# A gated two-layer expert kernel: weights loaded as blocks of adjacent rows, a half weight in a buffer of its own, and the work between the two expert layers rearranged

## The chip, the cores and the metric

One core of one Trainium2 chip. The metric is the device time of one execution in microseconds (us), the median of several runs. A profiled execution of the same kernel gives its own time, and the span from its first to its last instruction. Engine names: PE is the matrix engine (PEld its weight load), DVE the vector engine, ACT the scalar engine, POOL the third elementwise engine, SP the engine whose queue issues most of the transfers.

## The reference

Three parts run one after the other on 2304 tokens (4 batches of 576) of width 512.

```python
# 1: attention over the 32 largest scores of each row; 4 batches, 8 heads, 576 rows, 64 wide
scores = scale * q @ k.T ; keep the 32 largest of each row ; softmax ; attn @ v
# 2: soft mixture: 8 experts of 4 slots each (32 slots)
logits = x @ phi                              # 2304 x 32
d = softmax(logits, axis=0) ; slot_input = d.T @ x      # 32 x 512
for e in range(8):
    h = np.maximum(slot_input[e] @ w1[e], 0.0)          # 4 x 1024
    slot_out[e] = h @ w2[e]                             # 4 x 512
c = softmax(logits, axis=1) ; x = c @ slot_out          # 2304 x 512
# 3: gated mixture: the two best of 8 experts for each token
logits = x @ w_gate ; noise_scale = log1p(exp(x @ w_noise))
noisy = logits + noise_scale * noise ; top2, top2_w = two largest, their softmax
for e in range(8):
    h = np.maximum(x[mask] @ u1[e], 0.0) ; out[mask] += top2_w * (h @ u2[e])
```

(u1 and u2 stand for the third part's own w1 and w2, as in the kernel.) Each of the 32 weight matrices has 2 MB (512x1024 or 1024x512 float32).

## The kernel before, in words

*Attention* takes the first 420 us. It is one pipeline of 144 steps. During it five of the first weights are loaded in quarters, and the first half of the last w2 into `wz`.

*The soft mixture* (`moe`, lines 815 to 960): the eight w1 are read by PE as the wide operand (L860; 8 products of 4 column groups each for one expert), then the result `hs` is copied out of PSUM (L863 by ACT, L910 by DVE), turned (L851) and masked into `hM`. The eight w2 follow (L936; the last expert, in halves of the width, L940). Experts 0 to 6 add up in `sx`, which ACT copies to `sos`; the last one's two halves are added by DVE (L944). `sos` is turned and summed over the groups (L957) into `soT` (L964), the 32 slot outputs with their 512 features on partitions. `hs`, `hM` and `sos` all lie in the buffer `wb0`.

A contraction over 512 or 1024 rows goes in chunks of 128 rows, one row to a partition. Before, chunk c holds rows 128c to 128c+127: a partition's share of a weight is 4 pieces of 4 KB (w1, u1) or 8 pieces of 2 KB (w2, u2), taken from rows that lie 128 apart.

*The gates* (lines 1033 to 1111): `soT` times the gate weights (L1033), spread by group (`ggd`, L1038), times the softmaxed `c`, turned by `turn_c` into `ct` (L922, L923), gives the logits of all tokens (L1043). ACT and DVE work out the noisy logits and the two best (up to `mb`, L1079). PE counts positions (L1087 to L1093). Meanwhile PE multiplies `soT` with u1 of expert 0 (`weigh01`, L1004), since a token's input is a weighted sum of the 32 slot outputs. Where PE would wait it runs dummy products (`warm`, L846). Afterwards `gw`, the two gate weights of a token, are worked out (L1104, L1105 on DVE, L1108 on POOL), written into the rows `RW` and stored to the DRAM table `XD` (L1110), from which later experts fetch their tokens.

*The compaction* (`compact`, lines 1217 to 1238): for each of 18 token tiles a one-hot matrix is made, by DVE (L1231) or, for the tiles in `ONACT`, by two passes of ACT (L1226, L1227), and PE gathers expert 0's tokens with it (L1235). The first three quarters of u1 of expert 1 (`weigh01(1, c, P1)`) stand ahead of it on PE, the last quarter behind it. Then ACT rounds the first u2 (L1354), ACT and DVE copy the gathered tokens (`cts0`, L1256, L1257), and the first product of the gated experts can start (L1341, `first(0)`; it also needs `gs`, four small transfers issued by `stacked_g(0)`).

*The gated experts* (`gated`): 64 steps of products of three rounded parts (L1365 to L1367) until the end.

*Weight loads*: `order` lists the 32 weights, `slot` the buffer of each, `more(end)` issues the next loads as long as their buffer is free, `used` frees one. All go through SP's queue, in order: a load whose buffer is not yet free holds up whatever is behind it. Before, the loads around the change come in this order: w2 of experts 3, 4, 5, 6, the second half of the last w2 (into `wx1`), u1 of experts 0 and 1, the first quarter of u2 of expert 0, `gs`, the other quarters, u1 of experts 2 and 3, u2 of expert 1.

Of the kernel before, what the change touches and what calls it, by code (L numbers as in the profile page):

```python
# [34 lines left out]
ONACT = (7, 11, 15)  # L35
# [7 lines left out]
def moe_after_topk_attention(ctx: ExitStack, tc: tile.TileContext, q, k, v, phi, w1, w2, wg, wn, noise, u1, u2, qk, vt, qr, out):  # L43
# [3 lines left out]
    def pool(name, bufs=1, stack=ctx, **kw):  # L47
# [70 lines left out]

    def wload(i, part=None):
        m, e = order[i]  # L120
        h = homes[slot[i]]
        if (m, e) not in WT:
            WT[m, e] = wpool[h if h in wpool else h[:2]].tile([128, 4096], F32, name=h)
            held[slot[i]] = (m, e)
        if i == 15:
            whalf(1, WT[m, e][:, 0:2048])
            return
# [45 lines left out]


# [4 lines left out]
    def make_xtr(wk, xk, ps, soon, row, warm):  # L179
# [93 lines left out]
        def rest(b):  # L273
# [3 lines left out]
            A.copy(si[r], p[r])  # L277
# [35 lines left out]
        def last():  # L313
# [59 lines left out]
    def attention(st):  # L373
# [248 lines left out]
        def prepare():  # L622
# [3 lines left out]
            for i, w in enumerate((wg, wn)):  # L626
                at(40 + 2 * i, nc.sync.dma_start, wgn[:, :, 8 * i:8 * i + 8], w.rearrange("(c p) e -> p c e", p=128))
# [84 lines left out]
    def attention_check(st):  # L712
# [6 lines left out]
        c3 = st.tile([128, NT], I32, name="chk3")  # L719
# [95 lines left out]
    def moe(st, xp, xs, fast):  # L815
# [5 lines left out]
        for i in range(4):  # L821
            wpool[f"wy{i}"] = pool(f"wy{i}", 1, ta_st)
        tb = pool("tb", 1, tb_st, side="right")
# [32 lines left out]
        for e in range(E):  # L856
            w = WT[0, e].rearrange("p (c f) -> p c f", c=4)
            for n in range(2):
# [3 lines left out]
                if e == E - 1 and n == 0:  # L862
                    A.activation(hs[:, 0:512], h1[0], AF.Copy, scale=zs)  # L863
            used(0, e)
            more(20)
            if e == 5:
# [5 lines left out]
                if fast:  # L872
# [5 lines left out]
                    RW = tb.tile([128, 2, TT, ROW], F32, name="RW")  # L878
                    for c in range(2):
                        G.tensor_copy(RW[:, c, :, 0:NS], cn)  # L880
                        G.tensor_copy(RW[:, c, :, NS:NS + 1], ids.unsqueeze(2))
                        G.memset(RW[:, c, :, NS + 2:], 0.0)
# [27 lines left out]
        V.tensor_scalar(hs[:, 512:1024], h1[1], zs, None, op0=OP.mult)  # L910
# [7 lines left out]
        def turn_c():  # L918
            cf = cn.rearrange("p t s -> p (t s)")
            x = halves()  # L920
            for g in range(4):
                T.transpose(x[:, 0, g * 128:g * 128 + 128], cf[:, g * 128:g * 128 + 128], identf)  # L922
            T.transpose(x[:64, 1, :128], cf[:, 512:576], identf)  # L923
            A.copy(ct[:, 0:4], x[:, 0].rearrange("p (a b) -> p a b", a=4))
            A.copy(ct[:64, 4], x[:64, 1, :128])
# [3 lines left out]
        for e in range(E):  # L929
            w = WT[1, e].rearrange("p (c f) -> p c f", c=8)  # L930
            for n in range(2) if e == E - 1 else (None,):
                for c in range(8):
                    g = c % 4
                    o = slice(32 * g, 32 * g + 32)
                    if n is None:
                        T.matmul(sx[o], hM[:, e, c], w[:, c], start=(e == 0 and c < 4), stop=(e == E - 2 and c >= 4),  # L936
                                 tile_position=(0, 32 * g))
                    else:
                        x = wz.rearrange("p (c f) -> p c f", c=4)[:, c] if c < 4 else w[:, c - 4]
                        T.matmul(so[n][o, :256], hM[:, e, c], x[:, n * 256:n * 256 + 256], start=(c < 4), stop=(c >= 4),  # L940
                                 tile_position=(0, 32 * g))
                if e == E - 1:
# [36 lines left out]
        def stacked_g(e):  # L979
# [4 lines left out]
            for a in range(1, 4) if e == 0 else ():  # L984
                wload(18, a)
# [49 lines left out]
        if fast:  # L1035
            warm(2, "acc3")
# [8 lines left out]
        if fast:  # L1045
# [3 lines left out]
            warm(8, "acc2")  # L1049
# [54 lines left out]
        V.tensor_scalar(gw[:, 0], gw[:, 1], 1.0, 1e-9, op0=OP.add, op1=OP.add)  # L1104
        V.reciprocal(gw[:, 0], gw[:, 0])  # L1105
        wh_ = wpool["wx"].tile([128, 4096], F32, name="wx0")
        wf_ = wpool["wx"].tile([128, 4096], F32, name="wx1")
        G.tensor_tensor(gw[:, 1], gw[:, 1], gw[:, 0], op=OP.mult)  # L1108
# [548 lines left out]
```

## Time and profile before

| | us |
|---|---|
| median of 3 runs (741.35 to 742.44) | 741.62 |
| the profiled execution's own time | 739.92 |
| its span | 738.1 |
| PE busy in the span | 722.6 (98%) |
| DVE, ACT, POOL busy | 562.7, 484.8, 501.4 |

The time of the profiled execution is the span and 1.8 us around it. A busy time is the sum over an engine's instructions; PE's products are pipelined and their ends are modelled, and the dummy products count as busy, so 98% doesn't mean that PE does useful work in 98% of the time. "Idle before" in a row is the time that the engine stood still just ahead of it, with what ended it. The granted PE clock is 0.997 of full speed over the span.

### The profile page before, as it was taken

The numbers are of one execution on the slowest core, as the hardware profiler recorded it, in microseconds if no ns is written. First come the engines' busy times: TensorE is split into PE (matmuls) and PEld (weight loads), VectorE is DVE, ScalarE is ACT, GpSimd is POOL, SyncE is SP. The second block draws the span as 40 slices with busy tenths as digits, with TensorE's granted clock in tenths as the row PEclk, the third lists the DMA queues.
The fourth block names the chain that finished last, engine by engine and source line by source line (L and its number), as shares of the span: only waits on it lengthen the run. The fifth ranks groups of instructions, "written<-read, shape, count | busy, mean of one in ns | idle before, by whom it ended". The sixth has DMA issues, their size and how long they took to land.

```text
span 738.1 us, 17487 instructions
## 1 busy us (share of the span) xinstructions
PE 722.6 (98%) x5713; PEld 595.3 (81%) x5713; DVE 562.7 (76%) x2708; ACT 484.8 (66%) x1029; POOL 501.4 (68%) x656
## 2 busy tenths in 40 slices
PE   9999999999999999999999999999999999999995
PEld 4689999898999889998989634767876788888884
DVE  7999999999999998999987332978655656555561
ACT  5999999999999999999998302725222222322321
POOL 4999999998999999999877040436570527244044
PEclk9999999999999999999999999999999999999998
DMA  6147778776776543553376799999484986344055
GB/s 227 38 125 217 201 200 230 204 211 166 215 222 192 144 115 94 130 141 94 84 272 211 260 382 378 315 357 384 111 186 150 302 283 90 55 73 63 1 66 71
DMA packets 62326, 133.98 MB, mean 182 GB/s; under 512 B 13330, under 2 KB 14226, under 8 KB 62226
## 3 DMA queue, kind: packets, MB, share of 16 engines
q1 hardware_dynamic: 55042, 121.93, 54.3%
q0 software_dynamic: 7184, 10.85, 10.2%
q8 instruction: 47, 0.77, 0.4%
q14 instruction: 53, 0.43, 0.2%
HBM read 85.02 MB, written 17.97 MB: 140 GB/s over the span
## 4 chain that ended last, share of the span: by engine, by line
PE 53%; DVE 27%; POOL 8%; issue 5%; DMA 3%; ACT 2%; SPq 0%; POOLq 0%
DVE c L519 10%; PE acc L1365 9%; PE acc L1366 9%; PE acc L1367 9%; DVE TH L550 6%; PE av L586 5%; POOL u L542 4%; DVE c L526 4%; PE S L480 3%; DMA wx<-in_moe_w_dram 3%; PE st L562 3%; DVE mx L522 3%; PE hp L1341 2%; POOL s L557 2%; PE st L563 1%
## 5 line engine op out<-in xcount | busy, mean ns | idle before, releaser
L519 DVE MAX8 c<-s 128x8 f32<-128x82 f32 (+1 forms) x1008 | 222.2, 230 | 4.1 <-ACT s L499 3.5
L542 POOL TENSOR_TENSOR u<-g,s 128x576 f32<-128x576 bf16 x144 | 187.6, 1303 | 9.6 <-ACT g L536 9.6
L586 PEld LDWEIGHTS av<-vb,et 128*128 128x128 f32 (+1 forms) x1590 | 164.2, 180 | 11.2 <-issue 8.3
L586 PE MATMUL av<-vb,et 128*128 128x65 f32 (+1 forms) x1590 | 172.0, 263 | 0.8 <-ACT et L569 0.8
L1378 POOL DMA_INDIRECT out_dram<-y,ii x40 | 66.6, 1665 | 112.9 <-issue 60.3
L1346 ACT ACTIVATE hh<-hp 128x640 fp32r<-128x640 f32 x62 | 43.7, 705 | 136.1 <-PE hp L1341 132.6
L1365 PE MATMUL acc<-wh,hh 128*128 128x512 f32 x320 | 127.6, 399 | 0.8 <-DVE y L1375 0.7
L1366 PE MATMUL acc<-wl,hh 128*128 128x512 f32 x320 | 125.6, 393 | 0.0
L1367 PE MATMUL acc<-wh,hl 128*128 128x512 f32 x320 | 125.3, 392 | 0.0
L557 POOL TENSOR_SCALAR s<-s,mx 128x576 f32<-128x576 f32 x144 | 109.3, 759 | 21.3 <-ACT a L556 13.9
L550 DVE MAX8 TH<-u 128x8 f32<-128x584 f32 x144 | 109.2, 758 | 14.5 <-POOL u L543 13.6
L556 ACT ACTIVATE a<-s,TH 128x576 bf16<-128x576 f32 x144 | 117.6, 816 | 0.2
L536 ACT ACTIVATE g<-s,T 128x576 bf16<-128x576 f32 x144 | 116.6, 810 | 0.0
L562 PE MATMUL st<-identf,s 128*128 128x128 f32 x576 | 115.2, 280 | 1.3 <-POOL s L557 0.8
L1347 DVE SCALAR_TENSOR_TENSOR hl<-hp,hh 128x640 fp32r<-128x640 f32 x62 | 51.0, 823 | 75.1 <-ACT hh L1346 75.0
L563 PE MATMUL st<-steep,a 128*128 128x128 bf16 x576 | 105.5, 219 | 0.0
L480 PE MATMUL S<-ks,qs 128*128 128x288 f32 x560 | 105.1, 313 | 0.0
L501 ACT ACTIVATE s<-S 128x576 f32<-128x576 f32 x141 | 97.0, 688 | 4.8 <-PE S L490 2.8
L574 ACT ACTIVATE et<-st 128x512 f32<-128x512 f32 x144 | 90.6, 629 | 3.2 <-PE st L563 2.5
L562 PEld LDWEIGHTS st<-identf,s 128*128 128x128 f32 x576 | 83.5, 145 | 9.9 <-POOL s L557 3.3
L480 PEld LDWEIGHTS S<-ks,qs 128*128 128x128 f32 x560 | 78.6, 189 | 1.8
L1365 PEld LDWEIGHTS acc<-wh,hh 128*128 128x128 f32 x320 | 60.3, 189 | 15.1 <-issue 2.7
(368 smaller groups left out, 1158.1 us busy)
## 6 DMA issues: line engine op xcount, KB each, us to landing
wa<-in_moe_w_dram SPq DMA_DIRECT2D x8, 2048.0 KB, 13.4
wa<-in_moe_w_dram SPq DMA_DIRECT2D x28, 512.0 KB, 7.1
wb<-in_moe_w_dram SPq DMA_DIRECT2D x5, 2048.0 KB, 8.7
ks<-hl SPq DMA_DIRECT2D x56, 160.0 KB, 2.8
ks<-raw SPq DMA_DIRECT2D x56, 160.0 KB, 3.1
raw<-in_qk_dram SPq DMA_DIRECT2D x14, 608.0 KB, 4.2
wy<-in_moe_w_dram SPq DMA_DIRECT2D x4, 2048.0 KB, 10.6
wb<-in_moe_w_dram SPq DMA_DIRECT2D x16, 512.0 KB, 14.9
```

The source lines that it names most:

```text
L480: T.matmul(ph[hf][:, :288], QS[h][:, q0:q0 + 128], KS[h][:, l, ks], start=(n == 0), stop=(n == len(mm) - 1))
L519: V.max(C[i][:, c * 8:c * 8 + 8], SS[i][:, cut[c]:cut[c + 1]])
L536: A.activation(g, SS[i], AF.Sign, bias=last8(T24, i, 1), scale=-OVER, accum_out=SM[:, i:i + 1])
L542: G.tensor_tensor(u[:, 0:S], G1[i], SS[i], op=OP.mult)
L550: V.max(last8(TH, i), UU[i])
L556: A.activation(AP[i // 2][:, S * (i % 2):S * (i % 2) + S], SS[i], AF.Relu, bias=last8(TH, i, 1), scale=-1.0)
L557: G.tensor_scalar(SS[i], SS[i], -1.0, MX[i][:, 0:1], op0=OP.mult, op1=OP.add)
L562: T.matmul(o, SP[i // 2][:, ks], identf, start=True, stop=True, is_transpose=True)
L586: T.matmul(to[h][o:o + m, tt * 65:tt * 65 + 65], x, VB[j % 2][:, h, c if c < 4 else 4 + i % 2], start=(c == 0), stop=(c == 4), tile_positi ...
L1365: T.matmul(ACC[j], HH[n][:, r], WH[n], start=(c == 0), stop=False)
L1366: T.matmul(ACC[j], HH[n][:, r], WL[n], start=False, stop=False)
L1367: T.matmul(ACC[j], HL[n][:, r], WH[n], start=False, stop=(c == 7))
```

## The change

- Weights of w1, u1 and w2 are loaded in blocks of adjacent rows: of a block of 256 (w1, u1) or 512 rows (w2), partition p gets rows 2p and 2p+1, or 4p to 4p+3. A piece is then 8 KB. (The quarters loaded during attention stay at 4 KB; u2 keeps its layout.) w2 comes in two transfers instead of one.
- The other operand of each contraction has to follow that order of rows. The copies that already took it out of PSUM now deal it out: they read with a step of 2 or 4 elements (`dealt`, `taken`) in `rest`, in `last`, for `hs` and for `sos`. The gate weights are loaded in the same order, in two transfers each.
- The second half of the last w2 has a buffer of its own, `wv0` (8 KB of each partition), and is loaded right after w2 of expert 2. The last w2 is used first; the expert that is added in halves is now expert 6.
- u1 of experts 2 and 3 are loaded ahead of the first quarter of u2 of expert 0. u1 of expert 1 goes to `wx1`.
- `turn_c` is cut up: its transposes stand between the products that turn `sos` and behind L1033, in place of dummies.
- u1 of expert 1 is multiplied right behind that of expert 0, in place of eight dummies, and no longer around the compaction.
- `gw`, `RW`'s gate column and the store to `XD` come after the compaction. `RW` lies in `wb0` now, over `hM`, and is filled once `hM` is done with.
- `ONACT` is 8, 13, 17 instead of 7, 11, 15, with one scratch buffer `za` for all three. `ids_of(1)` comes two steps later.

```diff
-ONACT = (7, 11, 15)
+ONACT = (8, 13, 17)
...
-    order = ([(m, e) for m in range(2) for e in range(E)]
-             + [(2, 0), (2, 1), (3, 0), (2, 2), (2, 3), (3, 1), (2, 4), (2, 5), (3, 2), (2, 6), (2, 7)]
+    order = ([(0, e) for e in range(E)] + [(1, e) for e in (0, 1, 2, 7, 3, 4, 5, 6)]
+             + [(2, 0), (2, 1), (2, 2), (2, 3), (3, 0), (3, 1), (2, 4), (2, 5), (3, 2), (2, 6), (2, 7)]
...
-        f"wy{i}" for i in range(4)]
-    slot = [*range(11), 0, 1, 2, 3, 4] + [6, 0, 1, 2, 6, 5, 0, 2, 6, 1, 5] + [0, 2, 1, 5, 6]
+        f"wy{i}" for i in range(4)] + ["wv0"]
+    slot = [*range(12), 0, 1, 2, 3] + [6, 4, 0, 1, 2, 5, 6, 0, 1, 2, 5] + [6, 0, 2, 5, 1]
...
-            "(c p) f -> p c f", p=128))
+            "(p c) f -> p c f", p=128))
...
-        c = 4 if m % 2 == 0 else 8
-        n = 4 if m == 3 or part is not None else 1
-        d = WT[m, e].rearrange("p (c f) -> p c f", c=c)
-        s = (w1, w2, u1, u2)[m][e].rearrange("(c p) f -> p c f", p=128)
-        for a in range(n) if part is None else [part]:
-            cs = slice(a * c // n, (a + 1) * c // n)
-            nc.sync.dma_start(d[:, cs], s[:, cs])
+        s = (w1, w2, u1, u2)[m][e]
+        if h == "wv0":
+            whalf(1, WT[m, e])
+        elif m % 2 == 0:
+            d = WT[m, e].rearrange("p (a c f) -> p a c f", a=2, c=2)
+            s = s.rearrange("(a p c) f -> p a c f", a=2, c=2)
+            if part is None:
+                nc.sync.dma_start(d, s)
+            else:
+                nc.sync.dma_start(d[:, part // 2, part % 2], s[:, part // 2, part % 2])
+        else:
+            n = 2 if m == 1 else 4
+            d = WT[m, e].rearrange("p (a c f) -> p a c f", a=n, f=512)
+            s = s.rearrange("(a p c) f -> p a c f", a=n, p=128) if m == 1 else s.rearrange("(a c p) f -> p a c f", a=n, p=128)
+            for a in range(n) if part is None else [part]:
+                nc.sync.dma_start(d[:, a], s[:, a])
...
+    def dealt(x, a=1, c=2):
+        return x.rearrange("p (a c q) -> p a c q", a=a, c=c)
+
+    def taken(x, a=1, c=2):
+        return x.rearrange("p (a q c) -> p a c q", a=a, c=c)
...
-                copy(x[:, f], p[a][:, f])
+                copy(dealt(x[:, f]), taken(p[a][:, f]))
...
-                    A.activation(hs[:, 0:512], h1[0], AF.Copy, scale=zs)
+                    A.activation(dealt(hs[:, 0:512], 1, 4), taken(h1[0], 1, 4), AF.Copy, scale=zs)
...
-        V.tensor_scalar(hs[:, 512:1024], h1[1], zs, None, op0=OP.mult)
+        V.tensor_scalar(dealt(hs[:, 512:1024], 1, 4), taken(h1[1], 1, 4), zs, None, op0=OP.mult)
...
-        for e in range(E):
...
+        for e in (E - 1, *range(E - 1)):
...
-                    V.tensor_tensor(sos[:, f], so[n][:, 0:256], sos[:, f], op=OP.add)
-            if e == E - 2:
-                A.copy(sos, sx)
-                turn_c()
+                    V.tensor_tensor(dealt(sos[:, f]), taken(so[n][:, 0:256]), dealt(sos[:, f]), op=OP.add)
+            if e == E - 3:
+                A.copy(dealt(sos, 2), taken(sx, 2))
             used(1, e)
-            more(18 if fast else 20)
+            more(20)
         if fast:
-            wload(18, 0)
-            wnext[0] = 19
-        p = bank()
+            wload(20, 0)
+            wnext[0] = 21
+            RW = ww[:, F:F + 2 * TT * ROW].rearrange("p (c t f) -> p c t f", c=2, t=TT)
+            for c in range(2):
+                G.tensor_copy(RW[:, c, :, 0:NS], cn)
...
+        p, tc_ = bank(), halves()
         for c in range(4):
-            if c == 2 and fast:
-                warm(2, "acc3")
             T.matmul(p[:, c * 32:c * 32 + 32], sos[:, c * 128:c * 128 + 128], fold, start=True, stop=True)
+            if c == 1:
+                turn_c([0])
...
-        if fast:
-            warm(2, "acc3")
+        turn_c(range(1, 4))
...
-        if fast:
-            warm(2, "acc3")
+        turn_c([4])
...
-            warm(8, "acc2")
+            used(2, 0)
+            for c in range(4):
+                weigh01(1, c, P1)
+            used(2, 1)
...
-        used(2, 0)
-        more(21)
-        for c in range(3):
-            weigh01(1, c, P1)
         some(TT)
+        V.tensor_scalar(gw[:, 0], gw[:, 1], 1.0, 1e-9, op0=OP.add, op1=OP.add)
+        V.reciprocal(gw[:, 0], gw[:, 0])
+        G.tensor_tensor(gw[:, 1], gw[:, 1], gw[:, 0], op=OP.mult)
+        G.tensor_copy(RW[:, :, :, NS + 1], gw)
+        G.dma_start(XD[0:2 * NTOK].rearrange("(p r) f -> p (r f)", p=128), RW.rearrange("p c t f -> p (c t f)"))
         for e in (1, 0):
             slots_of(e)
-        weigh01(1, 3, P1)
-        used(2, 1)
```

## Rows read from the trace of the kernel before

**Rows 1.** The page: span, and PE's busy time with its share.
```profile
span 738.1 us, 17487 instructions
...
PE 722.6 (98%) x5713; PEld 595.3 (81%) x5713; DVE 562.7 (76%) x2708; ACT 484.8 (66%) x1029; POOL 501.4 (68%) x656
```

**Rows 2.** By stretch: start:end and length (us), PE busy (records), PEclk, DMA share, GB/s.
```profile
469.10:730.00 260.90, 259.89 (x1297) 1.00 0.64 168
```

**Rows 3.** The chain that ended last, in order of time: start, us, what.
```profile
428.37 19.36 DMA wx<-in_moe_w_dram
...
449.69 0.59 PE hp L922 x4
450.28 0.11 PE hp L923
...
452.82 0.43 PE acc L846 x2
...
453.61 0.43 PE acc L846 x2
...
454.44 0.54 PE acc L846 x2
454.98 1.32 PE acc L1043 x10
456.30 1.86 PE acc L1004 x32
458.16 1.83 PE acc L846 x8
...
468.56 0.57 PE tp L1004 x8
469.12 0.36 PE acc L1341
```

**Rows 4.** Timelines of PE (first row) and DVE: start, us, operation, count, idle before.
```profile
447.77 1.92 PE L936 MATMUL acc<-wx,wb 128*32 128x512 f32 x16 [0.21 <-DMA wx<-in_moe_w_dram]
...
452.32 0.42 DVE L944 TENSOR_TENSOR wb<-acc,wb 128x256 f32<-128x256 f32 x1 [0.37 <-PE acc L940]
...
454.52 0.22 DVE L1038 TENSOR_TENSOR ggd<-acc,group 128x64 f32<-128x64 f32 x1 [0.58 <-PE acc L1033]
...
459.41 0.31 DVE L1079 TENSOR_TENSOR mb<-T,nz 128x144 bf16<-128x144 f32 x1
...
499.67 0.59 DVE L1354 CAST wh<-wb 128x512 fp32r<-128x512 f32 x1
```

**Rows 5.** Timeline of ACT, around the end of the compaction.
```profile
466.61 0.74 ACT L1227 ACTIVATE wx<-wx 128x640 fp32r<-128x640 f32 x1
...
467.66 0.62 ACT L1354 CAST wh<-wa 128x512 fp32r<-128x512 f32 x1
468.45 0.43 ACT L1256 CAST cts<-acc 128x320 fp32r<-128x320 f32 x1 [0.16 <-PE acc L1235]
```

**Rows 6.** DVE groups by shape, 413 to 453 us: busy us, mean ns, idle before.
```profile
L325 DVE TENSOR_REDUCE mm<-st 1x32 f32<-1x160 f32 x1 | 0.3, 311 | 0.7 <-PE st L323 0.7
L910 DVE TENSOR_SCALAR wb<-acc,zs 128x512 f32<-128x512 f32 x1 | 0.8, 751 | 5.3 <-PE acc L860 5.3
```

**Rows 7.** By stretch, as rows 2: the transfers around the change.
```profile
419.00:423.00 4.00, 3.87 (x35) 1.00 0.16 58
439.00:447.00 8.00, 8.00 (x80) 1.00 1.05 386
450.00:457.00 7.00, 7.00 (x108) 1.00 1.03 421
461.00:465.00 4.00, 4.00 (x48) 1.00 0.58 151
```

**Rows 8.** Timeline of POOL.
```profile
462.41 1.01 POOL L1110 DMA_DIRECT2D xd<-RW  x1 [0.33 <-POOL RW L1109]
467.56 1.57 POOL L1158 TENSOR_SCALAR ge<-slot 128x18 f32<-128x18 f32 x6 [4.14 <-ACT slot L1229]
```

More of the change, by code (lines that the diff above doesn't have):

```diff
@@ L122, in wload @@
         if (m, e) not in WT:
-            WT[m, e] = wpool[h if h in wpool else h[:2]].tile([128, 4096], F32, name=h)
+            WT[m, e] = wpool[h if h in wpool else h[:2]].tile([128, 2048 if h == "wv0" else 4096], F32, name=h)
             held[slot[i]] = (m, e)
-        if i == 15:
-            whalf(1, WT[m, e][:, 0:2048])
-            return
-        c = 4 if m % 2 == 0 else 8
-        n = 4 if m == 3 or part is not None else 1
-        d = WT[m, e].rearrange("p (c f) -> p c f", c=c)
-        s = (w1, w2, u1, u2)[m][e].rearrange("(c p) f -> p c f", p=128)
-        for a in range(n) if part is None else [part]:
-            cs = slice(a * c // n, (a + 1) * c // n)
-            nc.sync.dma_start(d[:, cs], s[:, cs])
+        s = (w1, w2, u1, u2)[m][e]
[14 more added lines that the diff above has]
+                nc.sync.dma_start(d[:, a], s[:, a])
     def more(end, n=99):
@@ L276, in rest @@
             T.matmul(p[r], fold, SX[b], start=True, stop=True, tile_position=(0, 32 * b))
-            A.copy(si[r], p[r])
+            A.copy(dealt(si[r], 2), taken(p[r], 2))
         def merge1():
@@ L626, in prepare @@
             for i, w in enumerate((wg, wn)):
-                at(40 + 2 * i, nc.sync.dma_start, wgn[:, :, 8 * i:8 * i + 8], w.rearrange("(c p) e -> p c e", p=128))
+                for a in range(2):
+                    at(40 + 2 * i, nc.sync.dma_start, wgn[:, 2 * a:2 * a + 2, 8 * i:8 * i + 8],
+                       w[256 * a:256 * a + 256].rearrange("(p c) e -> p c e", c=2))
             for b in range(NB):
@@ L717, in attention_check @@
         V.scalar_tensor_tensor(c1, t24, 1.0, c1, op0=OP.is_lt, op1=OP.mult)
-        c3 = st.tile([128, NT], I32, name="chk3")
+        c3 = c2.bitcast(I32)
         V.tensor_scalar(c3, t24.bitcast(I32), 0x7fffff, None, op0=OP.bitwise_and)
@@ L822, in moe @@
             wpool[f"wy{i}"] = pool(f"wy{i}", 1, ta_st)
+        wpool["wv0"] = pool("wv0", 1, ta_st)
         tb = pool("tb", 1, tb_st, side="right")
@@ L877, in moe @@
                         G.tensor_copy(xw[:, :, 1, l], xw[:, :, 0, l])
[L878 to L882, printed above, removed]
             if e == 0:
@@ L916, in moe, with turn_c @@
         ct = tb.tile([128, 5, 128], F32, name="ct")
-        def turn_c():
+        def turn_c(gs):
             cf = cn.rearrange("p t s -> p (t s)")
[L920 to L925, printed above, removed]
+            for g in gs:
+                if g < 4:
+                    T.transpose(tc_[:, 0, g * 128:g * 128 + 128], cf[:, g * 128:g * 128 + 128], identf)
+                else:
+                    T.transpose(tc_[:64, 1, :128], cf[:, 512:576], identf)
+                if g == 3:
+                    A.copy(ct[:, 0:4], tc_[:, 0].rearrange("p (a b) -> p a b", a=4))
+                if g == 4:
+                    A.copy(ct[:64, 4], tc_[:64, 1, :128])
         sx, so = bank("acc2"), [bank(f"acc{n}") for n in range(2)]
         sos = ww[:, F + 2048:F + 2560]
-        for e in range(E):
-            w = WT[1, e].rearrange("p (c f) -> p c f", c=8)
-            for n in range(2) if e == E - 1 else (None,):
-                for c in range(8):
+        for e in (E - 1, *range(E - 1)):
+            if e == E - 1:
+                w = [x.rearrange("p (c f) -> p c f", c=4)[:, c] for x in (wz, WT[1, e]) for c in range(4)]
+            else:
+                w = [WT[1, e].rearrange("p (c f) -> p c f", c=8)[:, c] for c in range(8)]
+            for n, cs in ((0, range(4)), (1, range(4)), (0, range(4, 8)), (1, range(4, 8))) if e == E - 2 else (
+                    (None, range(8)),):
+                for c in cs:
                     g = c % 4
@@ L1103, in moe @@
         stacked_g(0)
[L1104 to L1105 removed]
         wh_ = wpool["wx"].tile([128, 4096], F32, name="wx0")
[L1107 to L1110 removed]
+        za = gp.tile([128, CAP], F32, name="za")
         idx = gp.tile([128, 2, TT], I32, name="idx")
@@ L1442, in gated @@
                 rows(1)
-                ids_of(1)
                 hots_of(t2, 0, (0, 1))
@@ L1452, in gated @@
                 rows(0)
+                ids_of(1)
                 ids_of(0)
```

17 lines of the change are left out of this document (8 added, 9 removed).

## The prediction, made before the changed kernel was built or run

> **What bounds the kernel now.** I read the page first: PE is busy in 722.6 of 738.1 us [rows 1]. That share can't be taken at its word, since dummy products count, so the next view is the chain that ended last [rows 3], and it shows three kinds of stretch. From 469.12 us on (the first product of the gated experts) PE works almost without a pause, 259.89 of 260.90 us [rows 2]; nothing in the change takes products out of that stretch, so it is moved as a block, and the question is by how much L1341 moves. Between the two expert layers, 447.77 to 469.12, the chain runs over short PE pieces, among them dummies (L846) and the transposes of `turn_c` (L922), and at its end over ACT. Ahead of 447.77 stands one long piece of DMA: the last full w2 (into `wx0`) landed 428.37 + 19.36 = 447.73. That looks like a transfer-bound stage, but PE's row there has only 0.21 us of idle time ahead of it [rows 4]; the two run level. The third view is the transfers by stretch [rows 7]: nearly nothing at 419 to 423 (58 GB/s), then full. Full means 386 GB/s where w2 in pieces of 2 KB moves and 421 GB/s where u1 in pieces of 4 KB does. At 461 to 465 it is down to 151 GB/s: there the next loads wait behind `gs`.
>
> So I sum what moves L1341, step by step along the chain, and then ask whether the transfers let it.
>
> **The sum, on PE's path**
>
> 1. `turn_c` leaves its old place: 0.59 + 0.11 [rows 3] = 0.70 us gained.
> 2. The wait for the last w2. `wv0`'s 1 MB goes out in the hole at 419 to 423 [rows 7] and no longer queues in the middle, and expert 6 is now used 1.8 us later. 0.2 us gained.
> 3. Turning `sos`. The second pair of L957 stood behind two dummies: 452.82 + 0.43 = 453.25 [rows 3]. DVE's sum that it needs ended 452.32 + 0.42 = 452.74 [rows 4]. With one transpose (0.59 / 4 = 0.15) in their place it starts at 452.97: 0.28 gained. The next two dummies (453.61, 0.43) become three transposes (0.45): nothing; they cover the copy of `soT`. Of the dummies behind L1033 (454.44, 0.54) one transpose remains, and L1043 is then held by `ggd`, ready at 454.52 + 0.22 = 454.74 [rows 4], where it started at 454.98: I take 0.1 of these 0.24, since a start follows a release by some 0.1 elsewhere. `ct`'s copies on ACT now start only after the third of these transposes; they take 0.59 and 0.26 by the length of the same operations before, and end some 0.2 ahead of need. 0.36 gained in all, 0 if that cover is gone.
> 4. Expert 1's products in place of eight dummies: as L1004's 32 records for expert 0, 1.86, against 1.83 [rows 3]. PE is free again at about the moment at which `mb` is ready (459.41 + 0.31 = 459.72 [rows 4]; PE's dummies end 459.99). 0.03 lost. Its weights must have landed by 458.16 - 1.26 = 456.9.
>
> PE's granted clock is 1.00 in all of rows 7; of the dummies that go, real products fill all but some 0.4 us, so I leave it there.
>
> Everything up to the position counts moves by 0.70 + 0.20 + 0.36 - 0.03 = 1.23. ACT's chain through the compaction hangs on those counts; still four copies of `gl` and three pairs, so it moves with them.
>
> 5. The end of the compaction. ACT ends its last pair at 466.61 + 0.74 = 467.35, rounds the first u2 from 467.66 (0.62), and then waited 0.16 for PE before `cts0` at 468.45 (0.43) [rows 5]. With the last tile on ACT and PE free of `weigh01(1, 3)`, PE has only that tile's two products to do behind ACT's last pair and is done before the rounding is. The 0.16 goes, and the 0.57 of L1004 at 468.56 [rows 3] with it, which only covered that copy. `cts0` then follows the rounding at once (468.28 instead of 468.45): 0.17 gained. DVE gives up the two `gw` operations ahead of its one-hots, but ACT ends last; nothing.
>
> 1.23 + 0.17 = 1.40 us.
>
> **What is moved elsewhere.** On POOL, filling `RW` (six short operations) moves to the end of the w2 products, where POOL has nothing to do; the `nt` that DVE needs for its one-hots is made behind it, some us ahead of need: nothing. `gw` and the store (1.01 [rows 8]) now stand ahead of `slots_of`, which began at 467.56; some 1.5 us later it still ends ahead of the joins on PE that read it, in steps 2 and 4 of the gated experts. The store lands later, about 473, but its first readers, the gathers of step 2, come after that. On SP the next load behind u2 of expert 0 is u2 of expert 1 into `wb0`, and it waits for that store; queued behind it are `gs` of expert 1 and u1 of experts 4 and 5. That u2 is first read at 499.67 [rows 4], over 25 us after the store, and its 2 MB take 5.4 at 386 GB/s: nothing.
>
> The strided copies: no row reads with a step of 2. The nearest is L325, which reads PSUM with a step of 32 elements: 311 ns for 160 elements [rows 6]; L944, contiguous, takes 0.42 for 256 [rows 4] and L910 751 ns for 512 [rows 6], the same 1.2 to 1.3 ns an element between them. So I take nothing for them. From below: no reason for a gain. From above: double the time for those on the path (the copy in `last`, as long as L944: 0.42; L910's 0.75; the second L944, 0.42), 1.6 us.
>
> On the layout in PSUM the Trainium skill speaks against the change: "SBUF — State Buffer", section "Door 1: The DMA port swizzle", says that PSUM has lines of 8 bytes, two fp32 values, and that a non-contiguous pattern slows matmuls significantly. It gives no price for a copy by DVE or ACT; L325's row shows none.
>
> **Do the transfers let it?** From `wv0` on, the queue is never empty until u2's first quarter and `gs` have landed. Before, the four w2 of experts 3 to 6 came first in it, and the last landed at 447.73; at 386 GB/s their 8.39 MB take 21.7, so that, with start-up and lag, they count from 426.0. With `wv0` running ahead there is less start-up, and I take 425.5. Then come 8 weights in pieces of 8 KB, 16.78 MB, and 0.52 MB each of u2's quarter (386 GB/s: 1.36) and `gs` (about 1.3). Needed: the quarter at 467.66 - 1.23 = 466.4, `gs` at 469.12 - 1.40 = 467.7.
>
> No row shows pieces of 8 KB. Bounds: 386 if they bring nothing over 2 KB, and 441 if the step from 386 to 421 is a fixed cost for a piece (5.31 ns for 2 KB and 9.73 for 4 KB over all engines: 0.88 fixed, so 18.6 for 8 KB). I take 430, between 4 KB's row and that.
>
> - 430: 39.0 us; the quarter lands 465.9, `gs` 467.2. In time by 0.5.
> - 421: 39.9; 466.8 and 468.1. L1341 0.4 late: gain 1.0.
> - 386: 43.5; 470.4 and 471.7. L1341 4.0 late: 2.6 lost.
>
> u1 of expert 1 is the sixth of the eight: at 430, 425.5 + 29.3 = 454.8, in time for 456.9.
>
> By the Trainium skill ("DMA: Bandwidth & Descriptors", section "Why small descriptors are slow (HBM only)") a descriptor pays some 3 cycles beside one for each 32 bytes; by that the step from 2 to 4 KB would be 2%. The rows show 9%, so the measurement decides. The estimate from that page for 8 KB is 1% over 421, and `gs` would land within 0.1 us of its need.
>
> **Forecast.** 739.92 - 1.40 = 738.5 for a profiled execution; the median of the runs lies 1.7 above the profiled one, 741.62 - 1.40 = 740.2.
>
> **Rivals**
>
> - *The transfers come late* (slower). u1 of experts 2 and 3 now stand ahead of u2's first quarter and of `gs`, 4.2 MB that came after them before. Whatever is missing in the rate is paid at ACT's rounding (L1354) and at L1341. It decides at about 410 GB/s: there 16.78 MB take 40.9, L1341 is 1.4 late, and the gain is gone. At 386: 744.2. For it: all 8 weights have to be through by 465, and the lag of the last pieces is only in my zero. Against it: 421 in the row for 4 KB. At 395, my value for this case, 3.0 late: 743.2.
> - *The strided copies cost double*: 1.40 - 1.6, 741.8, within 0.2% of no change. For it, that nothing before reads with these steps; against it, L325.
> - *Only part comes through*: ACT or `ggd` takes the place of the dummies (step 3 gone) and the transfers run at 421 or a little under: 741.0.
> - *More comes through*: the change also empties the queue in the first 50 us behind L1341, where PE's block has its few pauses (1.0 of 260.90 [rows 2]), and `ids_of(1)` no longer stands ahead of a gather on POOL. If all of that went: 739.2.
>
> **How the numbers follow.** A measurement of this kernel can tell about 0.2%, 1.5 us, from no change, so the forecast lies just inside "same". Chances: forecast 0.48 (739.7 to 740.7), part 0.16, more 0.14, late 0.15, strided copies 0.07. The range takes in everything from 739.0 (the last rival and 0.2 of scatter) to 743.2 (late transfers at 395). Faster by over 0.2% is below 740.1: all of "more" and 0.22 of the forecast's 0.48, 0.36. Slower is above 743.1: half of the late case, 0.08, and 0.05 for what I haven't seen, taken from the forecast's upper part: 0.13. The rest, 0.51, is same.
>
> **What would show it.** L1341 starts at 467.7 (forecast), or PE waits there for `gs`, or ACT ahead of its first rounding for `wa` (late). L940's products should start at once behind L936's, L957's pairs 0.15 apart, L1087 near 458.8 without a wait for expert 1's weights. L910's row should still say 0.75 and L944's 0.42. The stretch 439 to 447 should move some 430 GB/s. I'm wrong if the block behind L1341 changes its length by more than 0.5 us, or if the soft mixture or attention does.

## The result: slower by 0.5%, and the profile of the changed kernel

| | before | changed |
|---|---|---|
| median of 8 runs each, taken side by side, us | 741.14 (739.24 to 742.44) | 744.95 (743.38 to 746.63) |
| ratio, with its 95% interval | | 1.0051 (1.0034 to 1.0067) |
| the profiled execution, us | 739.92 | 746.63 |
| its span, us; mean granted PE clock | 738.1; 0.997 | 744.8; 0.990 |

The forecast was 740.2 us, in a range of 739.0 to 743.2. The change costs 3.8 us where 1.4 were to be gained. The line numbers of the changed kernel are larger by 10 to 21: L875 answers to L860, L920 to L910, L932 and L934 to L922 and L923, L936 to L924, L953 to L936, L956 to L940, L960 to L944, L975 to L957, L1002 to L983 (the transfers of `gs`), L1061 to L1043, L1023 to L1004, L1108 to L1087, L1251 to L1235, L1356 to L1341, L1369 to L1354, L1271 to L1256, L1380 to L1382 to L1365 to L1367. In the experiments they move by another 1 or 2: the gated products, L1356, are L1357 in e1, e8, e11 and e12 and L1354 in e5.

The page hardly moves ([rows 1] are the rows of before):

```profile
span 744.8 us, 17475 instructions
...
PE 723.6 (97%) x5699; PEld 596.7 (80%) x5699; DVE 562.5 (76%) x2708; ACT 485.1 (65%) x1029; POOL 500.1 (67%) x656
```

The chain that ended last, in order of time (start, us, what), tells more:

```profile
419.79 3.62 PE acc L875 x16
...
424.68 12.15 PE acc L875 x112
...
438.79 12.15 PE acc L953 x112
450.94 1.34 PE acc L956 x24
...
458.48 1.73 PE tp L1023 x32
...
463.76 9.51 DMA gs<-gl
...
473.41 1.41 PE acc L1356 x4
474.81 0.53 PE acc L1380
475.34 0.43 PE acc L1381
...
478.25 0.23 PE acc L1381
```

Three things are to be seen. The wait for the last w2, [rows 3], is gone: L953, L956 and what follows run without a transfer between them. In its place stands a transfer of 9.51 us, `gs`, that holds the first gated product until 473.41, where it began at 469.12 before. And the products behind that take 0.43 us each instead of 0.23 for some 4 us: PE's granted clock reads 0.50 at 473 to 477, the lower of its two levels (1.2 of 2.4 GHz; below).

The first line holds something that the change did not make. The 16 products took 3.62 us; before, the same 16 took 1.92, from 419.83 on. This half clock at 420 comes and goes from one execution to the next (last section), so from here on I compare starts by their distance from the first of these products, in executions where they took 1.92.

PE's timeline (start, us, line, operands, count, idle before) and ACT's rounding ahead of the gated products:

```profile
452.85 0.63 PE L975 MATMUL tp<-fold,wb 128*128 128x32 f32 x4 [0.19 <-DVE wb L960]
453.32 0.31 PE L932 MATMUL hp<-identf,LT 128*128 128x128 f32 x1
453.46 0.53 PE L975 MATMUL tp<-fold,wb 128*128 128x32 f32 x4
...
455.03 0.30 PE L934 MATMUL hp<-identf,LT 128*64 128x128 f32 x1 [0.21 <-ACT ct L936]
...
473.41 1.41 PE L1356 MATMUL acc<-cts,gs 128*128 128x320 f32 x4 [4.83 <-DMA gs<-gl]
```

```profile
470.15 0.62 ACT L1369 CAST wh<-wa 128x512 fp32r<-128x512 f32 x1 [1.78 <-DMA wa<-in_moe_w_dram]
```

Both transfers are late: ACT waits 1.78 us for u2's first quarter (`wa`), PE 4.83 us for `gs`. The transfers by stretch (length, busy time of each engine, PEclk, DMA share, GB/s) show the queue full all the way, where before it was down to 151 GB/s at 461 to 465 [rows 7]:

```profile
439.00:447.00 8.00, 8.00 (x80) 2.44 (x76) 0.12 (x1) 0.00 (x0) 0.88 (x3) 1.00 1.01 419
450.00:457.00 7.00, 6.58 (x107) 4.34 (x103) 1.32 (x5) 1.74 (x5) 1.90 (x7) 1.00 1.01 424
461.00:465.00 4.00, 3.98 (x24) 2.52 (x24) 3.89 (x11) 3.21 (x7) 0.00 (x0) 1.00 0.99 412
465.00:473.00 8.00, 3.58 (x21) 2.74 (x19) 4.37 (x11) 4.19 (x8) 4.06 (x13) 0.88 1.05 246
```

The last line is the odd one: from 465 to 473, while `gs` moves, the engines of the queue are as busy as ever (1.05) and move 246 GB/s instead of 420.

DVE's groups by shape (busy us, mean ns, idle before) show the strided copies, against L910's 751 ns of before [rows 6]:

```profile
L960 DVE TENSOR_TENSOR wb<-acc,wb 128x256 f32<-128x256 f32 x2 | 0.8, 424 | 13.3 <-PE acc L956 13.3
L920 DVE TENSOR_SCALAR wb<-acc,zs 128x512 f32<-128x512 f32 x1 | 0.8, 751 | 5.3 <-PE acc L875 5.3
```

### The profile page after: what moved, and what is told of

It reads as the page before. It is cut to its first block, busy times and chain, and to the rows that moved or that the text cites. A ratio compares the mean times of both kernels' runs of the same rounds, so it can differ in the third digit from the quotient of the medians.

```text
span 744.8 us, 17475 instructions
## 1 busy us (share of the span) xinstructions
PE 723.6 (97%) x5699; PEld 596.7 (80%) x5699; DVE 562.5 (76%) x2708; ACT 485.1 (65%) x1029; POOL 500.1 (67%) x656
## 4 chain that ended last, share of the span: by engine, by line
PE 54%; DVE 26%; POOL 9%; issue 6%; ACT 3%; DMA 1%; POOLq 0%; SPq 0%; ACTq 0%; DVEq 0%
DVE c L531 10%; PE acc L1380 9%; PE acc L1381 9%; PE acc L1382 9%; DVE TH L562 5%; PE av L598 5%; POOL u L554 4%; DVE c L538 4%; PE S L492 3%; PE hp L1356 2%; DVE mx L534 2%; PE st L574 2%; POOL s L569 2%; PE acc L875 2%; PE acc L953 2%
## 5 line engine op out<-in xcount | busy, mean ns | idle before, releaser
L1380 PE MATMUL acc<-wh,hh 128*128 128x512 f32 x320 | 128.2, 401 | 0.7 <-DVE y L1390 0.7
L1382 PE MATMUL acc<-wh,hl 128*128 128x512 f32 x320 | 125.7, 393 | 0.0
L1380 PEld LDWEIGHTS acc<-wh,hh 128*128 128x128 f32 x320 | 60.7, 190 | 15.0 <-issue 2.7
```

The source lines that it names most:

```text
L1380: T.matmul(ACC[j], HH[n][:, r], WH[n], start=(c == 0), stop=False)
L1382: T.matmul(ACC[j], HL[n][:, r], WH[n], start=False, stop=(c == 7))
```

## The experiments

The theory after reading the two traces: the chain is shortened as forecast, but u1 of experts 2 and 3, 2 MB each, now stand ahead of u2's first quarter and of `gs` in SP's queue; both come late, and the wait that this makes also lets PE's clock fall. Rivals: `gs` is slow because of what flows beside it, whatever the order; the blocks of rows or the strided copies cost the time; the half clock has another cause. Each ratio below is against the kernel before, run beside it.

**The order alone, undone (e1_u2_first).** The changed kernel with u2's first quarter and `gs` ahead of both u1.

```diff
-             + [(2, 0), (2, 1), (2, 2), (2, 3), (3, 0), (3, 1), (2, 4), ...
+             + [(2, 0), (2, 1), (3, 0), (2, 2), (2, 3), (3, 1), (2, 4), ...
...
-            wload(20, 0)
-            wnext[0] = 21
+            wload(18, 0)
+            wnext[0] = 19
...
+        more(21)
         some(TT)
```

(`slot`, not shown, gives the moved loads each other's buffers; so too in e4, e7 and e8.)

> The changed kernel, but with u2's first quarter of expert 0 and the four gs transfers ahead of u1 of experts 2 and 3, as in the kernel before; everything else as changed. Theory (what stands ahead in the queue): in the changed kernel the quarter landed at 470.1 us and gs at 473.3, because two weights (4.2 MB, 9.9 us at 424 GB/s) stood ahead. Here the quarter lands before 462 and gs by 468.5 (issued at 463 to 464, 3 to 5 us each as in the kernel before); the first product of the gated experts (L1341 in the kernel before, 469.1 there) starts at 467.7 to 468.5, or 1.7 later where PE's clock is low at the first w1 product, as it was in the profile of the changed kernel; no half clock at 471 to 478; time 739 to 741, 4 to 5 us under the changed kernel. Rival (gs is slow by itself): gs lands after 470 whatever stands ahead, and the time stays above 742.5. Rival (the loss is not there but in the clock at 420 us): the time falls by less than 2.5 us.

Measured: 740.54 us, ratio 0.9981 (0.9969 to 0.9994). PE's timeline:

```profile
457.84 0.24 PE L1108 MATMUL acc<-mb,before 128*128 128x144 bf16 x1
...
466.98 0.85 PE L1357 MATMUL acc<-cts,gs 128*128 128x320 f32 x4 [0.70 <-ACT cts L1272]
```

The first gated product waits for ACT's copy, as before, and for no transfer. From the first w1 product (419.19) to it are 47.79 us; before, 469.12 - 419.83 = 49.29. The shortened chain is worth 1.50 us, and it was the order of the loads that ate it. The measured time lies in the theory's range too.

**`gs` in another queue (e2_gs_on_pool).** The changed kernel with `gs` of expert 0 issued by POOL, so that it stands behind nothing in its own queue.

```diff
-                nc.sync.dma_start(g[32 * i:32 * i + 32].bitcast(F32), src[e // 4]...
+                (nc.sync if e else G).dma_start(g[32 * i:32 * i + 32].bitcast(F32), src[e // 4]...
```

> The changed kernel, with the four gs transfers of expert 0 issued from POOL's queue instead of SP's; u2's first quarter stays behind u1 of experts 2 and 3. Theory: gs no longer stands behind the weights; it shares the engines with them and lands by 469; the quarter still lands at about 470.1, so ACT's rounding (0.62) and its copy (0.43) hold the first gated product at about 471.3, 2 us earlier than in the changed kernel (473.4); time 742 to 743.5. Rival (gs is slow by itself, whichever queue): gs lands at 472 or later, the first product stays at 473 or later, time 744 to 746.

Measured: 747.12 us, ratio 1.0080 (1.0056 to 1.0103). The chain:

```profile
461.38 4.31 POOL gs L1002
465.69 6.91 DMA gs<-gl
...
472.74 1.40 PE acc L1356 x4
```

The theory's time is missed, and so is the rival's, though the rival's sign is there: `gs` lands behind 472, at 465.69 + 6.91 = 472.60. POOL is held for 4.31 us in the issue of the third transfer alone (last section), and then the last still takes 6.91 us, though nothing stands ahead of it in its own queue. So first in, first out is not all of it: `gs` is slow while the engines are full with weights. The Trainium skill has it so: "DMA: Bandwidth & Descriptors", section "Issuing engines are not separate DMA queues", says that transfers of all issuing engines share the same 16 DMA engines and interleave there. The 6.91 us agree. By the same starts the first gated product is 1.4 us later than in e9 below (472.74 - 419.40 = 53.34 against 51.96); why the median is 2.2 to 2.4 us above the changed kernel's stays open beyond that.

**The layout alone (e3_layout_only).** The kernel before with the blocks of rows and the dealt copies, and nothing else.

```diff
-        s = (w1, w2, u1, u2)[m][e].rearrange("(c p) f -> p c f", p=128)
...
+            s = s.rearrange("(a p c) f -> p a c f", a=2, c=2)
...
-            V.tensor_scalar(hs[:, 512:1024], h1[1], zs, None, op0=OP.mult)
+            V.tensor_scalar(dealt(hs[:, 512:1024], 1, 4), taken(h1[1], 1, 4), zs, None, op0=OP.mult)
```

> The kernel before with the row blocks alone: weights of w1, u1 and w2 in pieces of 8 KB and the copies that deal out; order, buffers, dummies and gates as before. Theory of the prediction: the transfers at 439 to 447 us move 420 to 430 GB/s instead of 386, the 0.2 us wait ahead of the last w2 goes, the strided copies last as long as the contiguous ones (0.75 and 0.42 us); the time is 0 to 0.5 us under the kernel before. Rival (strided copies double): up to 1.6 us over it.

Measured: 741.30 us, ratio 0.9993 (0.9980 to 1.0005): no change. The transfers run faster for it, 416 GB/s where before had 386 [rows 7], and PE waits for none of them between 440 and 480:

```profile
439.00:447.00 8.00, 8.00 (x77) 2.43 (x80) 0.29 (x1) 0.00 (x0) 2.58 (x10) 1.00 1.01 416
```

**One u1 ahead, in the kernel before (e4_one_u1_ahead).** The cause put into the kernel that doesn't have it: u1 of expert 2 ahead of u2's first quarter and `gs`.

```diff
-             + [(2, 0), (2, 1), (3, 0), (2, 2), (2, 3), (3, 1), ...
+             + [(2, 0), (2, 1), (2, 2), (3, 0), (2, 3), (3, 1), ...
...
```

> The kernel before with one change: u1 of expert 2 (2 MB) is loaded ahead of u2's first quarter of expert 0, and so ahead of gs. Theory (what stands ahead): the 2 MB take about 5 us at 421 GB/s; the quarter lands at 464 to 466 instead of 460, still in time for 467.7, and gs, issued at 460 to 464 behind it, lands at 468 to 471, so the first gated product (469.1) comes 0 to 2 us later; time 0 to 2 us over the kernel before. Rival (the queue ahead doesn't matter): no change.

Measured: 744.98 us, ratio 1.0042 (1.0027 to 1.0057). Chain, ACT and PE:

```profile
462.45 8.12 DMA gs<-gl
```

```profile
467.15 0.62 ACT L1354 CAST wh<-wa 128x512 fp32r<-128x512 f32 x1 [0.38 <-DMA wa<-in_moe_w_dram]
```

```profile
470.71 0.82 PE L1341 MATMUL acc<-cts,gs 128*128 128x320 f32 x4 [2.59 <-DMA gs<-gl]
```

One load moved, with nothing else of the change, makes a wait for `gs` too, and a half clock behind it (0.58 on the mean of 471 to 475), and costs nearly as much as the whole change. That is more than the 0 to 2 us that I had expected: the product comes 2.83 us later by the same starts (470.71 - 418.59 = 52.12 against 49.29), and I had left the clock out.

**What stands behind `gs`, held back (e5_quarters_held).** The changed kernel with quarters 1 to 3 of u2 issued by ACT after its copy of `cts`, not by SP right behind `gs`.

```diff
-            for a in range(1, 4) if e == 0 else ():
-                wload(20, a)
...
+        for a in range(1, 4):
+            wload(20, a, nc.scalar)
         split(0, hi=False)
...
```

> The changed kernel, except that quarters 1 to 3 of expert 0's u2, which SP issues right behind the four transfers of `gs`, are issued from ACT's queue only after ACT's cast of `cts`, so that nothing large stands behind `gs`. It tells why `gs` landed at 473.3. Theory (gs stands behind u1 of experts 2 and 3 and u2's first quarter, and then needs its own 2.5 to 5 us): the quarter still lands near 470 and the first gated product still starts at 472.5 to 473.5; after it the products of n = 2 to 6 may wait for the later quarters, so 744.5 to 748 us. Rival (gs is slow because the quarters behind it share its rings and engines): the first gated product starts by 471.0, at least 2 us earlier than the 473.41 of the changed kernel, with the quarter landing as before.

Measured: 743.01 us, ratio 1.0023 (1.0007 to 1.0040). PE's timeline:

```profile
469.86 1.41 PE L1354 MATMUL acc<-cts,gs 128*128 128x320 f32 x4 [3.46 <-DMA gs<-gl]
```

By the letter the rival's number came in, and the theory's time of 744.5 or more did not: the first gated product starts before 471.0. But 1.70 of the distance to 473.41 is the half clock at 420 of that one execution. Against e9 below, an execution of the changed kernel without it, it starts 1.42 us nearer to the first w1 product (469.86 - 419.32 = 50.54 against 471.67 - 419.71 = 51.96). The quarter itself moved by only 0.40 (ACT's rounding at 467.97 against 468.76, by the same starts). So both are true, in shares: against the 47.78 of e8 and 47.79 of e1, where no transfer is waited for, a wait of 2.8 us is left with nothing behind `gs`, and 1.4 come from the quarters behind it, as far as two single executions tell. In the wait that is left the queue is no longer full, by stretch as above:

```profile
465.00:467.00 2.00, 1.40 (x9) 0.93 (x7) 1.50 (x6) 1.15 (x4) 0.59 (x3) 1.00 0.69 120
467.00:469.00 2.00, 0.00 (x0) 0.00 (x0) 0.38 (x1) 0.94 (x2) 1.96 (x6) 0.90 0.55 203
```

**PE kept busy through the wait (e6_dummies_in_wait).** The changed kernel with 18 dummy products between the compaction and the first gated product.

```diff
+        p = ps.tile([128, 512], F32, name="acc0")
+        for _ in range(18):
+            T.matmul(p, onesb, onesb.unsqueeze(1).to_broadcast([128, 4, 128]), start=True, stop=True)
         first(0)
```

> The changed kernel with 18 dummy products (128x512, bf16, about 0.23 us each) put in TensorE's order between the compaction's last product and the first gated one, so that TensorE is busy while it waits for `gs`. It prices the half clock behind the wait by itself: in the changed kernel TensorE stood idle for 4.83 us and its clock was 0.50 from 473 to 477. Theory (the idle stretch is what lowers the clock, and that costs about 2 us of the loss): granted clock 1.00 from 471 to 479, gated products at 0.23 us instead of 0.43 from the first on, first gated product unmoved near 473.4, time 742.4 to 743.6, that is 1.4 to 2.5 us under the changed kernel. Rival (the half clock has another cause, or its cost is swallowed later by a wait for weights): 744.3 or more.

Measured: 744.50 us, ratio 1.0035 (1.0019 to 1.0051), against 1.0051 for the changed kernel on another chip. By the letter that is the rival's number, 744.3 or more. But the trace had the full clock from 467 to 479, as the theory asks, and the half clock at 420 (16 products in 3.29 us), so both kernels ran again on one chip.

> The changed kernel itself once more, on the same chip and in the same rounds as the next three, so that the half clock's price and the dose of u1 transfers can be read without a difference between chips. Expected from the trace of the changed kernel: 744.5 to 745.5 us, first gated product waiting 4 to 5 us for `gs`.

> The kernel of e6_dummies_in_wait beside e9. By e6's trace its gated block is 1.83 us shorter (743.3 - 473.74 against 744.8 - 473.41 us). Theory (that block is the price of the half clock): 1.3 to 2.3 us under e9. Rival (something after the block eats it, as the medians of e6 and of the changed kernel, 0.45 us apart on different chips, could mean): within 0.8 us of e9.

Measured: e9 744.68 us (ratio 1.0052, 1.0032 to 1.0071), e10 743.26 (1.0027, 1.0011 to 1.0044): 1.4 us apart, as the theory has it. The two intervals overlap, so the size is taken from the traces. PE's timelines, e9 first; these rows are the first three groups of gated products, so their distances are the time of the steps between them:

```profile
471.67 1.40 PE L1356 MATMUL acc<-cts,gs 128*128 128x320 f32 x4 [4.88 <-DMA gs<-gl]
475.52 0.74 PE L1356 MATMUL hp<-cts,gs 128*128 128x320 f32 x2
479.61 0.46 PE L1356 MATMUL hp<-cts,gs 128*128 128x320 f32 x2
```

```profile
471.49 0.83 PE L1356 MATMUL acc<-cts,gs 128*128 128x320 f32 x4 [0.87 <-DMA gs<-gl]
474.03 0.45 PE L1356 MATMUL hp<-cts,gs 128*128 128x320 f32 x2
477.73 0.46 PE L1356 MATMUL hp<-cts,gs 128*128 128x320 f32 x2
```

From the first to the third group e9 takes 7.94 us and e10 6.24, with the same start (51.96 and 51.86 us behind the first w1 product). The half clock costs 1.70 us, and nothing later eats it: to PE's last product (734.10 and 732.23) they take 262.43 and 260.74. The stretches of e9 show it (PEclk is the third number from the end), 0.61 and then 0.50 after PE's idle time of 4.88 us:

```profile
463.00:465.00 2.00, 2.00 (x13) 1.63 (x12) 2.00 (x6) 1.94 (x3) 0.00 (x0) 1.00 1.07 372
465.00:467.00 2.00, 1.79 (x11) 1.32 (x9) 1.57 (x6) 1.53 (x4) 0.47 (x2) 1.00 1.03 174
467.00:469.00 2.00, 0.00 (x0) 0.00 (x0) 0.32 (x1) 0.23 (x1) 1.69 (x5) 1.00 1.06 216
469.00:471.00 2.00, 0.00 (x0) 0.00 (x0) 0.71 (x1) 0.71 (x2) 1.69 (x6) 0.61 1.04 258
471.00:473.00 2.00, 1.33 (x5) 1.24 (x6) 0.16 (x1) 0.69 (x3) 1.99 (x8) 0.50 1.05 396
473.00:475.00 2.00, 2.00 (x6) 1.58 (x6) 2.00 (x5) 1.76 (x5) 1.69 (x5) 0.50 0.73 296
```

In e10 PEclk is 1.00 in every such stretch from 467 to 479.

**e1 with the old rows (e7_u2_first_old_rows).** The order of e1 and the shortened chain, but rows 128 apart, as before.

```diff
-            s = s.rearrange("(a p c) f -> p a c f", a=2, c=2)
+            s = s.rearrange("(a c p) f -> p a c f", a=2, c=2)
...
     def dealt(x, a=1, c=2):
-        return x.rearrange("p (a c q) -> p a c q", a=a, c=c)
+        return x
```

> The kernel of e1_u2_first (u2's first quarter and `gs` ahead of u1 of experts 2 and 3) without the blocks of rows: weights, `wg` and `wn` are read with rows 128 apart to a partition as in the kernel before, in pieces of 2 KB, and the copies are not dealt out. It tells whether e1's gain over the kernel before is the shortened chain alone. Theory (the chain is shortened by the same 1.3 us, the transfers have some microseconds to spare in this order, and the strided copies cost nothing): within 0.5 us of e1, 740.1 to 741.1. Rival (without the long pieces u2's first quarter or `gs` comes late again, or the weights of the first products do): first gated product waits for a transfer, 741.6 or more.

Measured: 741.55 us, ratio 0.9993 (0.9979 to 1.0006). PE's timeline, and the transfers:

```profile
458.60 1.93 PE L1022 MATMUL tp<-wx,soT 128*32 128x256 f32 x32 [0.63 <-DMA wx<-in_moe_w_dram]
```

```profile
439.00:443.00 4.00, 4.00 (x44) 1.21 (x40) 0.00 (x0) 0.00 (x0) 0.00 (x0) 1.00 1.05 386
```

I had expected e1's time; by the letter the measured one lies between the theory's range and the rival's. The first gated product waits for ACT, as in e1, but expert 1's products, brought forward by the change, wait 0.63 us for their u1, which with w2 at 386 GB/s comes too late. So the blocks do serve: they pay for the products in place of the dummies. The rest of the distance to e1 lies within the two intervals, and its trace had the half clock at 420 (16 products in 3.08 us), so how much the blocks are worth beyond 0.63 stays open.

**One u1 ahead, with the faster transfers (e8_one_u1_ahead_of_u2, e11, e12).** The changed kernel with u1 of expert 2 ahead and that of expert 3 behind.

```diff
-             + [(2, 0), (2, 1), (2, 2), (2, 3), (3, 0), (3, 1), ...
+             + [(2, 0), (2, 1), (2, 2), (3, 0), (2, 3), (3, 1), ...
...
```

> The changed kernel with only u1 of expert 2, not of expert 3, ahead of u2's first quarter and `gs`: the dose between e1_u2_first (none ahead, no wait) and the changed kernel (two ahead, first gated product at 473.41). One u1 is 1 MB (8 KB x 128 partitions), 2.4 us at the 430 GB/s of the windows. Theory (first in, first out): `gs` lands about 2.4 us earlier, near 470.9, against a need at about 468.5 with a cold start and 467.0 without one: the first gated product waits 1 to 3.5 us, with some half clock behind it, 742.0 to 744.0 us. Rival (the dose doesn't matter, since gs's slowness comes from whatever flows beside it): as the changed kernel, 744.5 or more; or no wait at all, 741 or less.

Measured: 738.76 us, ratio 0.9965 (0.9951 to 0.9979), with no wait for a transfer: the first gated product waits 0.70 us for ACT's copy, as in e1. By the letter that is the second half of the rival's number. My size was wrong: a u1 has 2 MB, not 1, and at 430 GB/s takes 4.9 us. With that, after the fact, the theory gives `gs` at 471.5 - 4.9 = 466.6 in e9's terms, ahead of the need at 467.5, and no wait, which is what came. In e4 the same place of u1 did make a wait; here the transfers are faster and `wv0`'s 1 MB is out of the way, and no run separates the two. e8 seemed better than e1, so both ran again side by side.

> The kernel of e8_one_u1_ahead_of_u2 beside e12. Theory (both have no wait ahead of the first gated product and the same chain, 47.78 and 47.79 us from the first w1 product to it, so they differ by chance alone, namely by which executions have a stretch of half clock): within 0.7 us of e12, and 1.0 to 2.7 us under the kernel before.

> The kernel of e1_u2_first beside e11. Rival to e11's theory (with both u1 late, products of experts 2 and 3 or the later weights wait somewhere behind the first gated product, which one u1 ahead avoids): 1 us or more above e11.

Measured: e11 740.05 us (ratio 0.9977, 0.9961 to 0.9993), e12 739.25 (0.9978, 0.9963 to 0.9994). They are alike: the ratios agree, and the medians, 0.80 us apart where I had said 0.7, lie the other way round than those of e1 and e8. Either order is the change without its fault, by the ratios 1.4 to 2.6 us faster than before in four measurements, and some 5 us faster than the changed kernel beside them (e9, 744.68).

## Why the prediction was wrong, step by step

**The chain (steps 1 to 5): right.** In the frame of before (first w1 product at 419.83) the position counts, L1108, start at 419.83 + 457.84 - 419.19 = 458.48 by e1; the forecast, 1.23 off the row of before below, is 458.60. From there to the first gated product are 9.14 us in e1 against 9.29 before: 0.15 gained, 0.17 forecast. (By the chain's starts, 457.91 and 460.00, the two parts are 1.45 and 0.05, so the split is good to 0.1.) The sum is 1.50, forecast 1.40.

```profile
459.83 0.23 PE L1087 MATMUL acc<-mb,before 128*128 128x144 bf16 x1
```

- Step 3 has its size but not its reason: the second four of L975 do start 0.14 behind the transpose (453.32, 453.46), but what L1061 waits for in the end is `ct`, 0.21 us, through the last transpose, and not `ggd`: the copies of `ct`, which were to end some 0.2 ahead of need, end behind it.
- The strided copies cost nothing: 751 ns and 424 ns, 751 [rows 6] and 0.42 us [rows 4] before. What the Trainium skill says of non-contiguous patterns in PSUM ("SBUF — State Buffer", section "Door 1: The DMA port swizzle") is said of matmuls; no run here shows it for copies by DVE with a step of 4 and of 2 elements.
- POOL's and SP's moves cost nothing that a wait shows.

**"Do the transfers let it?": wrong, by 4.3 us.** The rival *the transfers come late* happened, to which I gave 0.15. In e9, whose first w1 product starts 0.12 ahead of that of before, PE is let go at 471.67 and `gs` landed at 471.5 (9.55 us after its last issue at 461.98), forecast 467.2. What failed, by size:
- *The rate*, 430 GB/s taken, 412 to 424 measured in the rows above: 0.9 us by the prediction's own table. The step from 2 to 4 KB did not go on to 8 KB: 386, 421, and now 419 and 424.
- *The price of `gs`*, "about 1.3": a rate of weights put on a transfer that is no weight. Its four parts go from 32 partitions to 32 each. Where it runs with no weight beside it (e12, 457 to 464.5 us; queue, packets, MB, share of 16 engines' time) it takes 31.8% of 7.5 us for 0.52 MB:

```profile
q1 hardware_dynamic: 191, 0.52, 31.8%
```

That is 2.4 us for `gs`, 4.6 us a MB, against 2.4 us a MB for the weights in the changed kernel (3.33 MB at 100.3% of 8 us in 439 to 447). 1.1 us more than I took. The Trainium skill's "SBUF — State Buffer", section "Door 1: The DMA port swizzle", has a transfer's bandwidth hang on how many of SBUF's 16 ports its partitions reach; by its table 32 adjacent ones reach 8. Half of the 419 GB/s of the weights would be an estimate of 2.5 us; the row says 2.4, so the trace agrees. The trace of before had a hint of it: in 461 to 465 a share of 0.58 for 151 GB/s [rows 7] is 3.8 us a MB, mostly for `gs` and the store to `XD`. I read the GB/s of that row and not its share.
- *What stands behind it*: u2's other quarters, issued right behind `gs`, share its engines. 1.4 us by e5. It stood in the prediction as order only.

0.9 + 1.1 + 1.4 = 3.4 of the 4.3. The cause of the other 0.9 stays open. Part of the delay is there before `gs`: in e9 ACT's rounding is let go by u2's first quarter at 468.76, forecast 465.9, so a transfer that stands ahead of `gs` in the queue was 2.8 late, of which the rate and the quarters behind (0.4 by e5) explain 1.3. Nor is it a lack of engine time alone: in e5 the engines are busy 0.69 and 0.55 of the time while `gs` is still under way. The need was 467.5 in e9 (419.71 + 47.78, the chain of e8), so the wait is 4.2 us, 2.7 more than the chain had gained.

**The granted clock, "I leave it there": wrong as soon as there is a wait.** I asked only whether the dummies that go are replaced, not what a wait ahead of the gated products does. It costs 1.70 us by e9 and e10. My price for late transfers, 743.2 at 395 GB/s, lacked it, and so did the range. The sign that I had named, a block behind L1341 that changes its length by over 0.5 us, is there: 744.8 - 473.41 = 271.4 us against 738.1 - 469.12 = 269.0. PE's last products, before and changed, tell what it is made of:

```profile
729.85 0.39 PE L1367 MATMUL acc<-wh,hl 128*128 128x512 f32 x1
735.76 0.39 PE L1382 MATMUL acc<-wh,hl 128*128 128x512 f32 x1
```

Up to them it is 260.73 and 262.35 us, 1.6 more, about the half clock's price; 0.8 lie behind PE's last product. The sign was drawn too fine: the block of one and the same kernel takes 270.3 us in e1 and 269.5 in e12.

The sum of the mechanisms: -1.5 + 4.2 + 1.7 = +4.4 us; the medians say +3.8, and the second measurement +2.8 by the medians and +3.9 by the ratio. The profiled executions differ by 6.7 because that of the changed kernel has the half clock at 420 too (1.7), and 0.8 more behind PE's last product.

## What to carry to other kernels

A product brought forward is only worth its time if its weight comes forward too, and whatever the weight overtakes in the queue has to be priced at the far end: give the two or three transfers that the next stage needs first their place in the queue before filling it. Price a small transfer by the share of the engines that its own row shows, not by its bytes at the rate of large ones. And a wait on PE can cost more than its length: here 4.9 us of idle time drew 1.7 us of half clock behind it, and products that keep PE busy through the wait, though nobody needs them, took that away.

## What the runs showed of the hardware that I had not expected

The same kernel, in two executions, e8 and e11, at the first w1 products:

```profile
418.68 1.92 PE L875 MATMUL acc<-wa,siM 128*32 128x512 f32 x16
```

```profile
420.54 2.82 PE L875 MATMUL acc<-wa,siM 128*32 128x512 f32 x16
```

PE had been busy up to there in both, and in e11 its granted clock reads 0.50 at 419 to 421. Of the 14 profiled executions of this study (before, changed, e1 to e12) the 16 products took 2.8 to 3.6 us in 5 (changed, e3, e6, e7, e11) and 1.92 in 9, and the changed kernel has it in one execution and not in the other (e9), so it is not what the change costs; what brings it on was not found. On these 16 products alone it is 0.9 to 1.7 us, a good part of the spread between executions of one kernel: e11's twelve runs lie at 738.3 to 738.8 us with a mean clock of 0.996 to 0.997, and at 740.0 to 741.8 us with 0.993 to 0.994.

Issuing a transfer took POOL 0.49 to 0.75 us for three of the four of `gs` in e2 and 4.31 us for the other (shortest, median and longest, in ns):

```profile
L1002 POOL DMA_DIRECT2D gs<-gl x2: 492/2404/4317, 461.4 to 465.7; - x2
```

SP takes 0.51 to 0.58 us each for the same four, but it too was once held for 5.25 us by one issue, in the kernel before:

```profile
433.31 5.25 SPq L116 DMA_DIRECT2D wx<-in_moe_w_dram  x1
```

What holds up an issue that long stays open.
